# Second chunk's y read with its tokens regrouped, turned into a whole tile, and fetched back in four loads

## The chip, the cores and the metric

One core of a Trainium2 chip runs the kernel. The metric is device time in microseconds for one execution. The engines are TensorE (PE in the profile, its weight loads PEld), VectorE (DVE), ScalarE (ACT), GpSimd (POOL) and SyncE (SP, which in this kernel issues all DMA transfers). They run side by side, each in its own program order, and wait for one another through semaphores.

## The reference

A token mixer (sliding-window attention) times a gate from an MLP, over 2048 tokens of 512 features, all in float32:

```python
x = A_x                                   # 1 x 2048 x 512
xn = _layernorm(x, axis=-1)
s = _A_ref(xn, A_wqkv, A_wo)              # 32 heads of 16, window of 256 tokens, softmax, @ wo
g = _silu(_B_ref(xn, B_w1, B_b1, B_w2, B_b2))
return x + s * g

def _B_ref(x, w1, b1, w2, b2):
    y = _layernorm(x, axis=-1)
    h = _gelu(jnp.einsum("bsd,df->bsf", y, w1) + b1)      # 512 -> 1792
    return jnp.einsum("bsf,fd->bsd", h, w2) + b2          # 1792 -> 512
```

## The kernel before

**Stages.** The first 432 us or so are attention: 128 steps over 8 groups of heads and 16 blocks of keys, with the projections and the first chunk's hidden layer filled in between. Attention's unnormalised result goes to DRAM as `oT_d` (with the row of sums that the softmax divides by). Then the MLP and the output run over four chunks of 512 tokens. Chunks 0 and 1 are the loop `for c in range(2)`; chunks 2 and 3 are worked out together behind it, by another scheme.

**float32 products.** A product of two float32 matrices is made of three passes on TensorE: each operand is split into a high part and the rest (`gh` and `gl`, `yh` and the part in `xnT`, and so on). `split` makes them: a cast on ScalarE (or VectorE), then a subtraction on VectorE that needs the cast.

**The loop of a chunk.** Its 14 steps go over the 14 tiles f of 128 hidden units (in chunk 0 in the order 2, 3, 0, 1, 4, 5, 6 ... 13). In step i, ScalarE applies the gelu to tile `order[i]` and casts it to `gh`, VectorE subtracts for `gl` (`activate`, `split_g`), and PE projects the tile of the step before: four groups of `gh` x high, `gh` x low, `gl` x high (`project`, 12 matmuls into `acc`). `gh` and `gl` have two buffers each. In chunk 0 most hidden tiles exist already: 2, 3, 0 and 1 on the chip, 6 to 13 in DRAM (`h_d`, fetched as `hr`); 4 and 5 are made in the loop (`hidden`). The loop also settles late weights (`late_w`: casts and subtractions of `w` and `wos`, by the table `LATE`). After step 14 `end_chunk` adds the bias, applies the SiLU to `gated`, multiplies attention's four tiles `ohl` with `wos` on PE (48 matmuls `s`), and writes x + s * g out.

**y for the second chunk.** The MLP's input must stand with features in partitions and tokens along the row. Normalised x is in DRAM as `xn_d` (8 blocks of 128 tokens). Ahead of the loop, four loads bring chunk 1's blocks 4 to 7 into `y_1_0` ... `y_1_3` (pool `yp`, four buffers). In step 3 VectorE takes their statistics and POOL the power -1/2; in step 4 ScalarE normalises them in place, then `turn_y` transposes each tile on VectorE in place, in squares of 32 x 32, and sends it to DRAM (`z_d`). In step 5 `fetch_y` gathers for each quarter kt of the features four bands of 32 partitions: in each row, 16 pieces of 32 tokens, 128 bytes each. These 16 transfers land in `mlp["yy"][1][kt]` (part of `xnT`). Step 12 splits kt = 0 (its high part goes to `yh`), step 13 kt = 1, step 14 the other two. Chunk 1's hidden layer starts right behind `end_chunk`.

**Attention's tiles.** `fetch_sums` loads the softmax sums (`den`), steps 4 and 5 take reciprocals of them in four parts, step 5 writes them to DRAM (`rden_d`) and then calls `load_o` four times: a raw tile `or` of 8 heads (from `oT_d`, 8 slabs of 16 rows of 2 KB, into the buffers of pool `yp`) and its reciprocals, the `rec` (from `rden_d`, 8 rows, each repeated for 16 partitions; into a spare part of the `w2` area, in the profile `w`). Steps 9 to 12 multiply the two, steps 10 to 13 split the product into `ohl`.

**Order.** All engines but SP keep the order in which the program issues (`Ordered`), so every instruction carries line 43 in the profile, and tiles are told apart by their names. Inside the loop SP keeps that order too (`nc.sync.on = True`); elsewhere a scheduler may reorder SP. Eight semaphores serve SP's transfers in turn, so that one is issued only when the eighth before it has landed. DRAM areas are `dram.tile`s; a transfer that reads one waits for the ones that wrote it.

**Where in the code.** The loads of `y_1` are in line 872, `turn_y` in line 887, `fetch_y` in 894, `load_o` in 901, the loop from line 1081, step 4's transposes, step 5's transfers and the table of the splits from line 1124. Buffer `wa` of pool `bigp` holds `g_first` (the first two gelu tiles) until step 2 and `gated` from the end of chunk 0.

Of the kernel before, what the change touches and what calls it, by code (L numbers as in the profile page):

```python
# [9 lines left out]
F32 = mybir.dt.float32  # L10
# [7 lines left out]
S, D, H, DH, WIN, F = 2048, 512, 32, 16, 256, 1792  # L18
P = 128
NCH = S // 512  # L20
# [30 lines left out]
def mixer_kernel(ctx, tc, x, wqk, wv, wo, w1, b1, w2, b2, out):  # L51


    nc = SimpleNamespace(**{name: Ordered(tc, name) for name in ("tensor", "vector", "scalar", "gpsimd", "sync")})

    const = ctx.enter_context(tc.tile_pool(name="const", bufs=1))
    bigp = ctx.enter_context(tc.tile_pool(name="bigp", bufs=1))
    t2 = ctx.enter_context(tc.tile_pool(name="t2", bufs=5))
    small = ctx.enter_context(tc.tile_pool(name="small", bufs=3))
    dram = ctx.enter_context(tc.tile_pool(name="dram", bufs=1, space=bass.MemoryType.DRAM))  # L60
# [16 lines left out]
    def load(pool, tag, src, name, shape=(P, 512)):  # L77
        t = pool.tile(list(shape), F32, tag=tag, name=name)
        nc.sync.dma_start(t, src)
        return t  # L80
# [101 lines left out]
    xn_d = dram.tile([8, P, D], F32, name="xn_d")  # L182
    oT_d = dram.tile([4, 8, 32, S], F32, name="oT_d")
# [2 lines left out]
    w_d = {"w1": dram.tile([P, NF * 512], F32, name="w1_d"), "w2": dram.tile([P, NF * 512], F32, name="w2_d"),  # L186
           "wo": dram.tile([P, 4 * 512], F32, name="wo_d")}
    g_d = dram.tile([NF, P, 512], F32, name="g_d")
    z_d = dram.tile([NCH - 1, 4, P, 512], F32, name="z_d")
    mT_d = dram.tile([NQ, NCH, 32, P], F32, name="mT_d")  # L190


# [392 lines left out]
    mlp = {}  # L585
# [110 lines left out]
    n, raw = raws["qk"]  # L696
# [172 lines left out]
            nc.sync.dma_start(den[32 * g: 32 * g + 32], oT_d[g, :, DH].rearrange("a (c t) -> a c t", c=NCH))  # L869
        return den  # L870

    mlp["y"] = [load(mlp["yp"], "y", xn_d[4 + i], f"y_1_{i}") for i in range(4)]
    for f in range(6, NF, 2):
        t = gp.tile([P, 2, 512], F32, tag="ohl", name=f"hr_{f}", bufs=4)
        nc.sync.dma_start(t, h_d[f - 6: f - 4].rearrange("f p t -> p f t"))
# [11 lines left out]
    def turn_y(c, tiles):  # L887

        for i in tiles:
            y = mlp["y"][i]  # L890
            nc.vector.transpose(y, y)
            nc.sync.dma_start(z_d[c - 1, i], y)

    def fetch_y(c, kt, dst):

        for k in range(4):
            at = z_d[c - 1, 0, 0, 128 * kt + 32 * k: 128 * kt + 32 * k + 32]
            nc.sync.dma_start(dst[32 * k: 32 * k + 32].rearrange("p (t j) -> p t j", j=32),
                              bass.AP(tensor=at.tensor, offset=at.offset, ap=[[512, 32], [32 * 512, 16], [1, 32]]))

    def load_o(c, g):

        cols = slice(512 * c, 512 * (c + 1))
        pool, tag = (t2, "t2") if c else (mlp["yp"], "y")
        raw = load(pool, tag, oT_d[g, :, 0:DH, cols], f"or_{c}_{g}")
        rec = mlp["w2", g // 2][:, 512 * (14 + g % 2): 512 * (15 + g % 2)].bitcast(F32)
        nc.sync.dma_start(rec, bass.AP(tensor=rden_d.tensor, offset=rden_d.offset + 8 * g * S + 512 * c,
                                       ap=[[S, 8], [0, DH], [1, 512]]))
        return raw, rec

    def split_o(c, g, raw):
        ohl = gp.tile([P, 2, 512], F32R, tag="ohl", name=f"ohl_{c}_{g}", bufs=4)
# [168 lines left out]
    for c in range(2):  # L1081
        accs = open_accs(c)
        gs, os_, hs, wanted = {}, [], {}, []
# [22 lines left out]
        for i in range(NF + 1):  # L1106
            if i < NF:
                activate(order[i])
            if c and i in (1, 2, 6, 7):
                y_steps(6, 10)  # L1110
            if c and i >= 10 and i < 14:
                second_y(i - 10)
            if c and i == 14:
                kept["w"] = bigp.tile([P, 768], F32R, tag="wb1", name="wsh")
                combine_w(0)
            if c == 0:
                for kind, f in late_w[LATE[i]: LATE[i + 1]]:
                    settle(kind, f, nc.scalar.copy, nc.vector)
            if i >= 1:
                project(accs, [(order[i - 1], gs.pop(order[i - 1]))], order[0], order[-1])  # L1120
            if i + ahead < NF and order[i + ahead] not in made and order[i + ahead] > 1:
                hidden(order[i + ahead])
            if c == 0:
                if i == 3:
                    mlp["ln"] = layernorm(mlp["y"], "C1", True)
                    y_steps(0, 5)
                if i == 4:
                    y_steps(5, 10)
                    turn_y(1, range(4))
                if i in (4, 5):  # L1130
                    for j in (2 * i - 8, 2 * i - 7):
                        nc.vector.reciprocal(den[:, P * j: P * (j + 1)], den[:, P * j: P * (j + 1)])
                if i == 5:
                    nc.sync.dma_start(rden_d.rearrange("g a (c t) -> (g a c) t", c=NCH), den)
                    wanted += [load_o(0, g) for g in range(4)]
                    for kt in range(KT):
                        fetch_y(1, kt, mlp["yy"][1][kt].bitcast(F32))
                for kt in {12: (0,), 13: (1,), 14: (2, 3)}.get(i, ()):
                    split(mlp["yy"][0][kt], mlp["yy"][1][kt], mlp["yy"][1][kt].bitcast(F32))
            else:  # L1140
                steps2(i)
            k = i - o_from
            if 0 <= k - 2 - o_late < 4:
                os_.append(split_o(c, k - 2 - o_late, wanted[k - 2 - o_late][0]))
            if 0 <= k - 1 - o_late < 4:
                nc.vector.tensor_mul(wanted[k - 1 - o_late][0], *wanted[k - 1 - o_late])
            if c and 0 <= k < 4:
                wanted.append(load_o(c, k))
            if c == 0 and i == NF:
                mlp["y"] = load_y(2)  # L1150
            if c:
                if i in (2, 3, 7, 8):
                    turn_y(2 + i // 5, (0, 1) if i in (2, 7) else (2, 3))
                if i == 3:
                    mlp["y"] = load_y(3)
                    kept[0] = gated[:, 2:4]
                    kept[1] = bigp.tile([P, 2, 512], F32, tag="wb1", name="y2_21")
                    for kt in range(KT):
                        fetch_y(2, kt, kept[kt // 2][:, kt % 2])
                if i in (8, 9):  # L1160
                    for kt in (2 * i - 16, 2 * i - 15):
                        put("21" if kt > 1 else "11", kt % 2, kept[kt // 2][:, kt % 2])
                if i == 8:
                    fetch_second()
                if i == 12:
                    fetch_pair(0)
            if c and i in (0, 1, 5, 6):
                y_steps(5, 6)
# [110 lines left out]
    for i in range(NF):  # L1279
# [48 lines left out]
```

## Time and profile before

| | us |
|---|---|
| Time, median of 3 runs | 747.47 (745.95 to 747.61) |
| The profiled execution, its time | 746.98 |
| The profiled execution, span from first to last instruction | 745.2 |

| engine | busy, us | share of the span | instructions |
|---|---|---|---|
| PE | 728.8 | 98% | 7360 |
| PEld | 585.6 | 79% | 7360 |
| DVE | 516.5 | 69% | 790 |
| ACT | 440.1 | 59% | 744 |
| POOL | 297.5 | 40% | 644 |

TensorE's granted clock was 1.000 over the span, and 105.71 MB moved in 84,025 DMA packets.

How to read it: times count from the span's start. A row of a timeline has the start, the time from the first start to the last end of merged instructions, the engine, the operation, `out<-in` by the program's names, the number of instructions and, in brackets, the idle time before and who ended it. Rows with SPq are the issuing of transfers on SP, not the moving of data. A row of the windows has the length of the stretch, then for each engine busy time and instructions, then TensorE's clock, the share of the 16 DMA engines that were busy, and what they moved in GB/s. A row of the waits has who waited, for whom, the total, how often, and the longest.

### The profile page before, as it was taken

What the parts mean: (1) busy time and instruction counts of PE and PEld (TensorE: products, weight loads), DVE (VectorE), ACT (ScalarE), POOL (GpSimd) and SP (SyncE); (2) the same over time, 40 slices, a digit from 0 to 9 for tenths busy, and PEclk for the clock granted to TensorE, in tenths of its full rate; (3) what the DMA queues carried; (4) which work ended last, traced back from release to release, by engine and by line L of the source; (5) the groups of instructions that cost most, each with busy time, mean ns of one, the idle gap of its engine ahead of it and who ended that gap; (6) DMA issues with size and microseconds to landing.
All of it is one profiled execution on the core that took longest, in us unless ns stands there. A gap on an engine that the chain in (4) does not pass through costs nothing.

```text
span 745.2 us, 18812 instructions
## 1 busy us (share of the span) xinstructions
PE 728.8 (98%) x7360; PEld 585.6 (79%) x7360; DVE 516.5 (69%) x790; ACT 440.1 (59%) x744; POOL 297.5 (40%) x644
## 2 busy tenths in 40 slices
PE   8999999999999999999999999999999999999997
PEld 7886777777778887777776688788888888888886
DVE  6886777877766678887773567656658755676643
ACT  7757767867667676778877756443544734442001
POOL 7413757757666555767867700020102000001102
PEclk9999999999999999999999999999999999999999
DMA  8633355757555624646735385745453322253611
GB/s 289 192 71 77 86 137 149 210 151 194 142 133 153 154 71 149 163 129 165 201 103 161 92 286 201 198 143 194 110 108 113 96 88 74 69 181 117 214 55 56
DMA packets 84025, 105.71 MB, mean 142 GB/s; under 512 B 36640, under 2 KB 36896, under 8 KB 83936
## 3 DMA queue, kind: packets, MB, share of 16 engines
q1 hardware_dynamic: 83936, 104.50, 49.5%
q8 instruction: 58, 0.95, 0.5%
q14 instruction: 31, 0.25, 0.1%
HBM read 54.53 MB, written 32.77 MB: 117 GB/s over the span
## 4 chain that ended last, share of the span: by engine, by line
PE 86%; ACT 5%; DVE 3%; DMA 2%; issue 1%; POOL 1%; SPq 1%; DVEq 0%; ACTq 0%; POOLq 0%
PE fb L43 19%; PE acc L43 17%; PE zo L43 12%; PE stb L43 9%; PE p L43 9%; PE s L43 6%; PE h L43 6%; PE xy L43 5%; ACT pt L43 4%; PE pv L43 3%; POOL pt L43 1%; DVE xy L43 1%; SPq L43 1%; DMA w<-rden_d 1%; DMA xnT<-z_d 1%
## 5 line engine op out<-in xcount | busy, mean ns | idle before, releaser
L43 POOL TENSOR_SCALAR_AFFINE_SELECT pt<-pt 128x256 f32<-128x256 f32 x480 | 192.9, 425 | 133.7 <-ACT pt L43 131.7
L43 ACT ACTIVATE pt<-stb 128x768 f32<-128x768 f32 (+1 forms) x244 | 188.5, 773 | 62.4 <-PE stb L43 55.1
L43 DVE TENSOR_REDUCE mt<-xy 128x4 f32<-128x1024 f32 (+1 forms) x128 | 152.6, 1192 | 4.4
L43 DVE COPY_PREDICATED xy<-upper,zo 128x512 f32<-128x512 int32 x112 | 77.8, 695 | 70.6 <-PE xy L43 63.1
L43 POOL TENSOR_TENSOR xo<-xo,gated 128x512 f32<-128x512 f32 x15 | 19.9, 1330 | 236.9 <-DVE gated L43 195.5
L43 PE MATMUL fb<-xnT,wqb 64*128 64x512 f32 (+1 forms) x684 | 104.6, 397 | 0.2
L43 PE MATMUL zo<-pt,vt 128*17 128x128 f32 x2880 | 103.7, 275 | 0.3 <-POOL pt L43 0.3
L43 PE MATMUL stb<-qk 64*128 64x384 f32 (+1 forms) x488 | 97.1, 393 | 6.2 <-ACT pt L43 3.9
L43 PE MATMUL acc<-w,gh 128*128 128x512 f32 x320 | 98.6, 389 | 0.4 <-ACT gh L43 0.4
L43 PEld LDWEIGHTS stb<-qk 64*128 64x128 f32 x488 | 45.8, 183 | 51.5 <-ACT pt L43 46.3
L43 PEld LDWEIGHTS zo<-pt,vt 128*17 128x17 f32 x2880 | 67.5, 97 | 15.6 <-issue 6.3
L43 PEld LDWEIGHTS fb<-xnT,wqb 64*128 64x128 f32 (+1 forms) x684 | 64.7, 185 | 11.0 <-DVE pjr L43 1.4
L43 PEld LDWEIGHTS acc<-w,gh 128*128 128x128 f32 x320 | 60.0, 188 | 13.1 <-ACT gh L43 0.8
L43 PE MATMUL acc<-w,gl 128*128 128x512 f32 x160 | 62.3, 390 | 1.0 <-DVE gl L43 1.0
L43 PE MATMUL xy<-qk 64*128 64x256 f32 (+2 forms) x536 | 58.4, 291 | 0.2
L43 PEld LDWEIGHTS xy<-qk 64*128 64x128 f32 x536 | 46.6, 185 | 6.6 <-issue 3.1
L43 ACT COPY oraw<-zo 128x128 f32<-128x128 f32 x128 | 34.0, 266 | 29.4 <-PE zo L43 28.7
L43 PE MATMUL s<-wos,ohl 128*128 128x512 f32 (+1 forms) x204 | 44.3, 376 | 0.0
L43 ACT ACTIVATE gated<-acc 128x512 f32<-128x512 f32 x16 | 8.7, 596 | 59.3 <-DVE acc L43 59.3
L43 PEld LDWEIGHTS s<-wos,ohl 128*128 128x128 f32 x204 | 36.8, 188 | 7.1
L43 PEld LDWEIGHTS zo<-qk 64*128 64x128 f32 x448 | 38.5, 185 | 4.6 <-issue 1.4
L43 ACT COPY p<-p 128x512 f32<-128x512 f32 x21 | 12.3, 585 | 48.9 <-PE p L43 41.2
(191 smaller groups left out, 1233.8 us busy)
## 6 DMA issues: line engine op xcount, KB each, us to landing
qk<-sh SPq DMA_DIRECT2D x128, 128.0 KB
qk<-pjr SPq DMA_DIRECT2D x64, 128.0 KB
oT_d<-oraw SPq DMA_DIRECT2D x32, 256.0 KB
w_d<-in_w_dram SPq DMA_DIRECT2D x14, 512.0 KB
x<-in_x_dram SPq DMA_DIRECT2D x16, 256.0 KB
or<-oT_d SPq DMA_DIRECT2D x16, 256.0 KB
w<-rden_d SPq DMA_DIRECT2D x16, 256.0 KB
xo<-in_x_dram SPq DMA_DIRECT2D x16, 256.0 KB
```

Of the source, the lines that this page charges most:

```text
L43: r = issue(*args, **kwargs)
```

## The change

The four loads of `y_1` take other tokens together: tile i has rows 32 i to 32 i + 31 of each of the blocks 4 to 7, so that partition 32 a + t holds token 128 a + 32 i + t of the chunk. The four transposes write into one tile `whole`, in buffer `wa`, in which partition 32 a + p has, for each band b of 32 features, the 128 tokens of block a in a row. Four transfers, one for each a, write it to `zt_d`, whose rows are features and whose columns are tokens, in pieces of 128 tokens (512 bytes). Four whole loads of 128 rows of 2 KB bring `mlp["yy"][1]` back, in place of the 16 gathers.

SP's order in step 5 becomes: the four writes, the four raw tiles, `rden_d`, the four loads of y, the four `rec`. Before, it was the writes (in step 4), `rden_d`, raw and `rec` in turn four times, the 16 gathers. The split of kt = 0 moves from step 12 to step 9. Behind the loop, SP's built order mixes the next chunk's four `y` loads with the four `xo` loads (y, xo, y, xo, xo, y, xo, y; before, the four `y` came first). On ACT and DVE nothing else moves, and PE's and POOL's orders are as before. Chunks 2 and 3 use `turn_y` and `fetch_y` as before, with `z_d` now for two chunks.

```diff
-    z_d = dram.tile([NCH - 1, 4, P, 512], F32, name="z_d")
+    z_d = dram.tile([2, 4, P, 512], F32, name="z_d")
+    zt_d = dram.tile([S // 4, 512], F32, name="zt_d")
...
-    mlp["y"] = [load(mlp["yp"], "y", xn_d[4 + i], f"y_1_{i}") for i in range(4)]
+    mlp["y"] = [load(mlp["yp"], "y", xn_d[4: 8, 32 * i: 32 * i + 32], f"y_1_{i}") for i in range(4)]
...
-    def load_o(c, g):
-
-        cols = slice(512 * c, 512 * (c + 1))
+    def load_raw(c, g):
+
         pool, tag = (t2, "t2") if c else (mlp["yp"], "y")
-        raw = load(pool, tag, oT_d[g, :, 0:DH, cols], f"or_{c}_{g}")
+        return load(pool, tag, oT_d[g, :, 0:DH, 512 * c: 512 * (c + 1)], f"or_{c}_{g}")
+
+    def load_rec(c, g):
+
         rec = mlp["w2", g // 2][:, 512 * (14 + g % 2): 512 * (15 + g % 2)].bitcast(F32)
         nc.sync.dma_start(rec, bass.AP(tensor=rden_d.tensor, offset=rden_d.offset + 8 * g * S + 512 * c,
                                        ap=[[S, 8], [0, DH], [1, 512]]))
-        return raw, rec
+        return rec
+
+    def load_o(c, g):
+        return load_raw(c, g), load_rec(c, g)
...
                 if i == 4:
                     y_steps(5, 10)
-                    turn_y(1, range(4))
+                    whole = bigp.tile([P, 16, 4, 32], F32, tag="wa", name="y_1")
+                    for j, y in enumerate(mlp["y"]):
+                        nc.vector.transpose(whole[:, :, j], y.rearrange("p (b t) -> p b t", t=32))
...
                 if i == 5:
+                    for a in range(4):
+                        nc.sync.dma_start(zt_d[:, P * a: P * (a + 1)].rearrange("(b p) t -> p b t", p=32),
+                                          whole[32 * a: 32 * a + 32].rearrange("p b i t -> p b (i t)"))
+                    first_o = [load_raw(0, g) for g in range(4)]
                     nc.sync.dma_start(rden_d.rearrange("g a (c t) -> (g a c) t", c=NCH), den)
-                    wanted += [load_o(0, g) for g in range(4)]
                     for kt in range(KT):
-                        fetch_y(1, kt, mlp["yy"][1][kt].bitcast(F32))
-                for kt in {12: (0,), 13: (1,), 14: (2, 3)}.get(i, ()):
+                        nc.sync.dma_start(mlp["yy"][1][kt].bitcast(F32), zt_d[P * kt: P * (kt + 1)])
+                    wanted += [(first_o[g], load_rec(0, g)) for g in range(4)]
+                for kt in {9: (0,), 13: (1,), 14: (2, 3)}.get(i, ()):
                     split(mlp["yy"][0][kt], mlp["yy"][1][kt], mlp["yy"][1][kt].bitcast(F32))
```

More of the change, by code (lines that the diff above doesn't have):

```diff
@@ L891, in turn_y @@
             nc.vector.transpose(y, y)
-            nc.sync.dma_start(z_d[c - 1, i], y)
+            nc.sync.dma_start(z_d[c - 2, i], y)
     def fetch_y(c, kt, dst):
         for k in range(4):
-            at = z_d[c - 1, 0, 0, 128 * kt + 32 * k: 128 * kt + 32 * k + 32]
+            at = z_d[c - 2, 0, 0, 128 * kt + 32 * k: 128 * kt + 32 * k + 32]
             nc.sync.dma_start(dst[32 * k: 32 * k + 32].rearrange("p (t j) -> p t j", j=32),
                               bass.AP(tensor=at.tensor, offset=at.offset, ap=[[512, 32], [32 * 512, 16], [1, 32]]))
-    def load_o(c, g):
-        cols = slice(512 * c, 512 * (c + 1))
+    def load_raw(c, g):
         pool, tag = (t2, "t2") if c else (mlp["yp"], "y")
-        raw = load(pool, tag, oT_d[g, :, 0:DH, cols], f"or_{c}_{g}")
+        return load(pool, tag, oT_d[g, :, 0:DH, 512 * c: 512 * (c + 1)], f"or_{c}_{g}")
+    def load_rec(c, g):
         rec = mlp["w2", g // 2][:, 512 * (14 + g % 2): 512 * (15 + g % 2)].bitcast(F32)
```

## The prediction, made before the changed kernel ran

> **What bounds the kernel now.** I read the page first (busy time, chain of waits), then the timeline of PE around the change.
>
> ```profile
> span 745.2 us, 18812 instructions
> PE 728.8 (98%) x7360; PEld 585.6 (79%) x7360; DVE 516.5 (69%) x790; ACT 440.1 (59%) x744; POOL 297.5 (40%) x644
> ...
> PE 86%; ACT 5%; DVE 3%; DMA 2%; issue 1%; POOL 1%; SPq 1%; DVEq 0%; ACTq 0%; POOLq 0%
> ```
>
> PE is busy for 98% of the span, so the change can win only where PE waits, and lose wherever it makes PE wait. The timeline of PE in the loop of the first chunk (c = 0):
>
> ```profile
> 446.16 0.61 PE L43 MATMUL acc<-w,gh 128*128 128x512 f32 x2
> ...
> 452.05 0.39 PE L43 MATMUL acc<-w,gl 128*128 128x512 f32 x1
> ...
> 465.65 0.39 PE L43 MATMUL acc<-w,gl 128*128 128x512 f32 x1
> ...
> 473.88 0.73 PE L43 MATMUL acc<-w,gh 128*128 128x512 f32 x2 [0.36 <-ACT gh L43]
> 475.60 0.50 PE L43 MATMUL acc<-w,gl 128*128 128x512 f32 x1 [0.98 <-DVE gl L43]
> ...
> 478.00 11.04 PE L43 MATMUL s<-wos,ohl 128*128 128x512 f32 x48
> ```
>
> Each f takes twelve matmuls, one every 0.227 us (the 48 of 11.04 us), so 2.72 us; the third one needs gl. From 446.16 eleven such groups follow (f = 1, 4, 5, ... 13). Without waits the last would end at 446.16 + 11 x 2.72 = 476.1; the `s` matmuls start at 478.0. PE loses 1.9 us, all at f = 13. The timeline of ACT names the cause, the arrival of the second chunk's turned y (lines of 128 bytes from z_d):
>
> ```profile
> 471.93 0.62 ACT L43 CAST yh<-xnT 128x512 fp32r<-128x512 f32 x1 [3.37 <-DMA xnT<-z_d]
> ```
>
> ACT and DVE run in order, so gh and gl of f = 13 stand behind this cast and its subtraction. **The most that the change can win is therefore these 1.9 us.**
>
> **What is removed.** SP's timeline shows what was queued, in order:
>
> ```profile
> 430.11 0.52 SPq L43 DMA_DIRECT2D oT_d<-oraw  x1
> ...
> 431.42 2.61 SPq L43 DMA_DIRECT2D y<-xn_d  x4
> ...
> 437.42 2.84 SPq L43 DMA_DIRECT2D den<-oT_d  x4
> 440.32 1.04 SPq L43 DMA_DIRECT2D hr<-h_d  x2
> ...
> 443.88 1.76 SPq L43 DMA_DIRECT2D wos<-wo_d  x4
> 447.10 2.44 SPq L43 DMA_DIRECT2D z_d<-y  x4
> 453.69 0.32 SPq L43 DMA_DIRECT2D rden_d<-den  x1
> ...
> 461.19 15.22 SPq L43 DMA_DIRECT2D xnT<-z_d  x16
> ```
>
> Sixteen reads, 15.2 us of SP, become four, at the 0.44 us of one wos load some 1.8 us. If the four land before the casts at i = 13 and 14, the wait at f = 13 goes: minus 1.9.
>
> **What is moved at the front: the y loads.** Same four transfers of 256 KB, but each now gathers 32 rows from each of four slabs (4 x 32 x 512) instead of 128 rows in a line. The trace before has reads of such a shape: or<-oT_d and w<-rden_d gather 16 rows from each of eight slabs. Busy time by windows (the last two columns are the share of the 16 DMA engines, and GB/s):
>
> ```profile
> 447.50:451.50 4.00, 4.00 (x19) 3.31 (x18) 4.00 (x7) 3.29 (x6) 0.00 (x0) 1.00 1.05 400
> 461.25:462.25 1.00, 1.00 (x6) 0.81 (x5) 0.82 (x2) 0.29 (x1) 0.00 (x0) 1.00 0.47 180
> 497.00:498.00 1.00, 1.00 (x6) 0.80 (x6) 0.02 (x1) 0.00 (x0) 0.90 (x1) 1.00 0.50 190
> 474.00:477.00 3.00, 2.02 (x8) 1.36 (x9) 2.96 (x6) 1.19 (x2) 0.00 (x0) 1.00 0.80 125
> ```
>
> With whole 128-row transfers queued (447.5) all engines work, at 400 GB/s. With only eight-slab reads queued, several at once, half of them work, at 180 to 190. So eight slabs go to eight engines, the same eight for each transfer. I take it that four slabs go to four engines, a quarter of the rate: 262 KB at 100 GB/s is 2.62 us a load instead of 0.66. The only four-slab transfer in the rows, oT_d<-oraw, speaks for it: SP waits for it before den, so 256 KB took from 430.11 to 437.4. The bounds for the four loads are 2.6 us (all engines) and 10.5 us; I take 10.5, **7.9 us later** for the last.
>
> The row shows eight slabs only; from it alone the four loads might run on four different quarters, side by side, and cost nothing (first rival, 745.6). [...]
>
> Who waits: DVE's statistics of y at i = 3, with gl of f = 4 and all else queued behind them. SP's waits between 430 and 450, then DVE, then POOL:
>
> ```profile
> SPq L43 <- DMA y<-xn_d: 0.2, 1, 0.2
> ```
>
> ```profile
> 441.77 0.66 DVE L43 BATCH_NORM_STATS2 bnC<-y 128x6 f32<-128x512 f32 x1
> ...
> 442.68 0.17 DVE L43 TENSOR_SCALAR veC<-mvC 128x4 f32<-128x4 f32 x1
> 444.11 0.69 DVE L43 TENSOR_TENSOR gl<-g,gh 128x512 fp32r<-128x512 f32 x1 [1.26 <-ACT gh L43]
> ...
> 445.32 0.15 DVE L43 SCALAR_TENSOR_TENSOR shiftC<-mvC,rsC 128x4 f32<-128x4 f32 x1
> 446.36 2.83 DVE L43 STREAM_TRANSPOSE y<-y 128x512 f32<-128x512 f32 x4 [0.89 <-ACT y L43]
> ...
> 450.76 0.63 DVE L43 TENSOR_TENSOR gl<-g,gh 128x512 fp32r<-128x512 f32 x1
> ...
> 461.91 0.69 DVE L43 TENSOR_TENSOR or<-or,w 128x512 f32<-128x512 f32 x1 [0.18 <-issue]
> 463.15 0.69 DVE L43 TENSOR_TENSOR gl<-g,gh 128x512 fp32r<-128x512 f32 x1 [0.55 <-ACT gh L43]
> ```
>
> ```profile
> 442.94 1.02 POOL L43 TENSOR_TENSOR rsC<-veC,mhalf 128x4 f32<-128x4 f32 x1 [16.33 <-DVE veC L43]
> ```
>
> SP's short wait on a y load ended just before it issued hr at 440.32; one load further (0.66) the last y was in, about 441.0, at the latest 441.77. With 7.9 more: T = 448.9. The chain from there, by these rows' distances: veC at T + 0.9, the power on POOL done at T + 2.2, gl of f = 4 and the subtraction of w (444.11 to 445.32, 1.2 us) meanwhile, the shift at T + 2.3 = 451.2 instead of 445.32, 5.9 late. The normalisation on ACT, the four transposes, the reciprocals and gl of f = 5 follow without a gap to give way: gl starts at 456.7, is done at 457.3, and PE wanted it at 452.05. **First stall: 5.2 us** (4.4 to 6.0 with the landing between 0.8 earlier and later).
>
> **The transposes** (0.71 us each) now write sixteen blocks of 128 bytes at a stride instead of in place. No row shows that; from no difference up to twice the time (2.8 us, all on the chain above). I take none: element count and engine are the same. The buffer of `whole` held g_first, last read by PE long before; the next owner, gated, is written after 478. Both free.
>
> **The writes.** Pieces of 512 bytes, 1 MB in all. 128-byte pieces run at 125 GB/s with the engines 0.80 busy, 2 KB pieces at 400: 1 MB is 8.4 us by the one and 2.6 by the other. In time of one engine a piece costs 0.80 x 16 x 128 B / 125 GB/s = 13 ns and 1.05 x 16 x 2048 B / 400 GB/s = 86 ns; a straight line between gives 28 ns for 512 bytes, 2048 pieces on 16 engines **3.5 us**. [...]
>
> **SP's new order.** The raws pass rden_d, but the reciprocals' loads (rec, w<-rden_d) now stand behind the four y reads, which stand behind the landing of the writes. The first rec releases or_0's product, at i = 9, and gl of f = 10 is queued behind it. On the four slow engines, after T = 448.9: hr 2.1 MB, den 0.26, b2s 0.26, wos 1.05, 3.7 MB at 400 GB/s 9.2 us; the writes 3.5; four raws at 185 GB/s (eight slabs) 5.7; rden_d 0.7; y reads 2.6; the first rec 1.4. That ends at 472.0. The chain of waits has what a landing takes beyond its data:
>
> ```profile
> 453.69 1.98 DMA rden_d<-den
> ...
> 455.68 6.14 DMA w<-rden_d
> ```
>
> rden_d, 0.66 of data, took 1.98; half of the 1.3 beyond comes after the data: rec lands at 472.6 instead of about 461.8. Product (0.6) and gl (0.7) end at 473.9. PE wants gl of f = 10 at 465.65 + 5.2 = 470.9. **Second stall: 3.0 us**; from 0 (a queue 3 us shorter) to 7.9 (writes at the 128-byte price, 4.9 more).
>
> **The split moved from i = 12 to i = 9** (one ACT cast, one DVE subtraction): its y is in at about 469.5, three us after ACT wants it, but gh of f = 10 is then done near 471.4, inside the second stall, so nothing on top. Were rec early, it would cost 0.6. At the loop's end the next chunk's x and xo loads go out in mixed order; the 11 us of `s` matmuls hide them, without that cover 0.7 each.
>
> **Sum.** The profiled execution took 746.98 (span 745.2 and 1.8 around it), the median of the runs is 747.47, 0.5 above. 746.98 + 5.2 + 3.0 - 1.9 = 753.3; with the 0.5, **753.8**.
>
> **Rivals.**
> 1. The four loads spread over all engines, or over different quarters: place, the statistics of y at i = 3; price, nothing in place of 8.2. It decides if the last y lands by 443.7 (a shift up to 0.66 late is free, since gl of f = 5 was done at 451.4 and wanted at 452.05). Only the gain stays: 747.47 - 1.9 = 745.6, not slower. For it: no row shows a four-slab read. Against it: 0.47 and 0.50.
> 2. Only the first stall: the queue is 3 us shorter and rec arrives in time. 747.47 + 5.2 - 1.9 = 750.8. For it: engines other than the four slow ones have room. Against: a transfer lands when its slowest engine is done.
> 3. The 512-byte writes cost as much per byte as 128-byte pieces: second stall 7.9, 758.7. For it: 125 GB/s is the only row with small pieces. Against: those are reads, 16 engines only 0.80 busy.
>
> **How the numbers follow.** Forecast 0.53, rival 1 0.12, rival 2 0.18, rival 3 0.17. A change under 0.3% (2.2 us) can't be told from none here. Rival 1's 1.9 lies just within that: 0.07 same, 0.05 faster; the others, 0.88, are slower. The range runs from rival 2 with its early landing (750.8 - 0.8, rounded down) to rival 3: 749.8 to 758.7; it leaves out rival 1 and what goes past rival 3.
>
> **What would show it.** Right: during the y loads, the DMA share falls towards 0.25; the last statistics start near 449; PE waits for gl of f = 5 about 5 us; or_0's product waits for w<-rden_d; no wait is left at f = 13. Wrong: statistics near 442, or a first rec in before 465 with PE still late. The forecast fails altogether if four slabs do not mean four engines.

## The result, and the profile after

| | us |
|---|---|
| Before, median of 4 runs beside the changed kernel | 747.54 (745.95 to 748.28) |
| After, median of 4 runs | 757.30 (756.74 to 759.23) |
| Ratio, with its 95% interval | 1.0138 [1.0114, 1.0163] |
| The profiled execution after, its time | 756.74 |
| Its span | 755.0 |

The change makes the kernel slower by 9.8 us (1.4%). The prediction said 753.8 us. The page of the kernel after, the span, busy times and the chain of waits:

```profile
span 755.0 us, 18773 instructions
PE 733.9 (97%) x7360; PEld 588.5 (78%) x7360; DVE 517.4 (69%) x790; ACT 439.8 (58%) x744; POOL 297.9 (39%) x644
...
PE 82%; DMA 5%; ACT 4%; DVE 3%; issue 2%; POOL 2%; SPq 1%; DVEq 0%; ACTq 0%; POOLq 0%
...
PE fb L43 17%; PE acc L43 17%; PE zo L43 11%; PE p L43 9%; PE stb L43 9%; PE s L43 6%; PE h L43 5%; PE xy L43 5%; ACT pt L43 4%; PE pv L43 3%; DMA y<-xn_d 2%; SPq L43 1%; POOL pt L43 1%; DMA rden_d<-den 1%; DVE xy L43 1%
```

PE has the same 7360 matmuls, and its busy time grows by 5.1 us: some of them take longer. DMA's share of the chain went from 2% to 5%, with y<-xn_d and rden_d<-den now in it by name. The timeline of PE after, at the places where it waited in the loop of chunk 0:

```profile
451.00 0.50 PE L43 MATMUL acc<-w,gl 128*128 128x512 f32 x1 [2.02 <-DVE gl L43]
451.34 0.89 PE L43 MATMUL acc<-w,gh 128*128 128x512 f32 x2
...
456.26 0.73 PE L43 MATMUL acc<-w,gh 128*128 128x512 f32 x2 [1.11 <-ACT gh L43]
457.98 0.50 PE L43 MATMUL acc<-w,gl 128*128 128x512 f32 x1 [0.99 <-DVE gl L43]
...
475.50 0.79 PE L43 MATMUL acc<-w,gl 128*128 128x512 f32 x1 [2.03 <-DVE gl L43]
...
487.63 11.04 PE L43 MATMUL s<-wos,ohl 128*128 128x512 f32 x48
```

There are waits at f = 4 and 5 (451 to 458; I call them the first wait, after the first stall of the prediction), one at f = 10 (475.50, the second wait), and none at f = 13, where the kernel before lost 1.9 us. The `s` matmuls start at 487.63 instead of 478.00. What the waits end on, by the timelines of DVE and ACT after:

```profile
440.35 0.69 DVE L43 BATCH_NORM_STATS2 bnC<-y 128x6 f32<-128x512 f32 x1 [1.42 <-DMA y<-xn_d]
443.57 0.69 DVE L43 BATCH_NORM_STATS2 bnC<-y 128x6 f32<-128x512 f32 x1 [2.31 <-DMA y<-xn_d]
446.59 0.69 DVE L43 BATCH_NORM_STATS2 bnC<-y 128x6 f32<-128x512 f32 x1 [2.11 <-DMA y<-xn_d]
449.23 0.69 DVE L43 BATCH_NORM_STATS2 bnC<-y 128x6 f32<-128x512 f32 x1 [1.72 <-DMA y<-xn_d]
...
452.90 2.83 DVE L43 STREAM_TRANSPOSE y<-y 128x512 f32<-128x512 f32 x4 [0.88 <-ACT y L43]
...
457.29 0.63 DVE L43 TENSOR_TENSOR gl<-g,gh 128x512 fp32r<-128x512 f32 x1
...
474.15 0.69 DVE L43 TENSOR_TENSOR or<-or,w 128x512 f32<-128x512 f32 x1 [2.13 <-DMA w<-rden_d]
474.76 0.69 DVE L43 TENSOR_TENSOR gl<-g,gh 128x512 fp32r<-128x512 f32 x1
```

```profile
470.68 0.62 ACT L43 CAST yh<-xnT 128x512 fp32r<-128x512 f32 x1 [2.12 <-DMA xnT<-zt_d]
```

The four y tiles come in one after another, 2.6 to 3.2 us apart, the last at 449.23. The windows show what the DMA engines did meanwhile: three stretches after, in which SP had nothing issued behind the y loads (its next issue, hr, begins at 434.79 and is held until 439.8), then the stretch of the same loads before:

```profile
436.00:437.00 1.00, 1.00 (x6) 0.84 (x5) 0.61 (x2) 0.97 (x3) 0.00 (x0) 1.00 0.26 100
438.00:439.00 1.00, 1.00 (x6) 0.84 (x5) 0.93 (x2) 0.05 (x1) 0.00 (x0) 1.00 0.26 102
439.00:440.00 1.00, 1.00 (x7) 0.81 (x6) 0.00 (x0) 0.00 (x0) 0.00 (x0) 1.00 0.26 100
```

```profile
431.50:441.00 9.50, 9.50 (x44) 7.85 (x43) 6.30 (x13) 5.76 (x11) 0.00 (x0) 1.00 0.82 270
```

A share of 0.26 is the work of four of the 16 engines (0.26 x 16 = 4.2), at 100 GB/s together. Gl of f = 5 is queued behind their normalisation and starts at 457.29. At f = 10 gl is queued behind the first product of attention's tile, which waits for its `rec` until 474.15. The chain of waits names the transfers:

```profile
433.73 15.48 DMA y<-xn_d
...
462.39 7.66 DMA rden_d<-den
...
470.11 3.95 DMA w<-rden_d
```

The last y load took 15.48 us from issue to landing. `rden_d`, issued at 462.39 behind four raw tiles, landed 7.66 us later, and only then was the first `rec` issued. Besides the two waits there is a third cost, the clock. The windows after, behind the waits and between them (the column after POOL is TensorE's granted clock):

```profile
451.30:454.50 3.20, 3.20 (x9) 2.52 (x8) 2.01 (x5) 2.45 (x4) 0.52 (x1) 0.53 0.97 312
458.30:461.60 3.30, 3.30 (x9) 2.61 (x8) 3.03 (x5) 0.84 (x2) 0.00 (x0) 0.51 0.87 235
462.00:472.80 10.80, 10.80 (x49) 8.95 (x48) 4.57 (x7) 6.74 (x12) 0.00 (x0) 1.00 0.76 228
476.00:478.60 2.60, 2.60 (x7) 1.98 (x7) 2.56 (x5) 0.00 (x0) 0.00 (x0) 0.50 0.58 189
```

PE is busy all through 476.0 to 478.6 but does 7 matmuls, one in 0.43 us (476.10 to 476.95 is two), where 0.227 was the rule. The clock is halved three times for 3.4 us: behind the wait of 2.02 us, behind those of 1.11 and 0.99 us together, and behind that of 2.03 us. In the kernel before it stayed at 1.00 behind the wait of 0.98 us.

So the loss is made up like this. The first low product of f = 10 ran at 465.65 before and at 475.50 after, 9.85 us later. From there to `s` the kernel before took 12.35 us, of which 1.9 were waits at f = 13, so 10.45 without them. The kernel after has no wait there and takes 12.13 us: 1.9 less for the waits and 1.68 more. Nine matmuls behind the second wait, 475.50 to 479.20, account for the 1.68: they took 3.70 us, and at 0.227 each they would have taken 2.04. Together 9.85 - 1.9 + 1.68 = 9.63, the lateness of `s`.

### The profile page after: what moved, and what is told of

It reads as the page before. It is cut to its first block, busy times and chain, and to the rows that moved or that the text cites. A ratio compares the mean times of both kernels' runs of the same rounds, so it can differ in the third digit from the quotient of the medians.

```text
span 755.0 us, 18773 instructions
## 1 busy us (share of the span) xinstructions
PE 733.9 (97%) x7360; PEld 588.5 (78%) x7360; DVE 517.4 (69%) x790; ACT 439.8 (58%) x744; POOL 297.9 (39%) x644
## 4 chain that ended last, share of the span: by engine, by line
PE 82%; DMA 5%; ACT 4%; DVE 3%; issue 2%; POOL 2%; SPq 1%; DVEq 0%; ACTq 0%; POOLq 0%
PE fb L43 17%; PE acc L43 17%; PE zo L43 11%; PE p L43 9%; PE stb L43 9%; PE s L43 6%; PE h L43 5%; PE xy L43 5%; ACT pt L43 4%; PE pv L43 3%; DMA y<-xn_d 2%; SPq L43 1%; POOL pt L43 1%; DMA rden_d<-den 1%; DVE xy L43 1%
## 5 line engine op out<-in xcount | busy, mean ns | idle before, releaser
L43 PE MATMUL acc<-w,gh 128*128 128x512 f32 x320 | 102.1, 401 | 1.1 <-ACT gh L43 1.1
L43 PEld LDWEIGHTS acc<-w,gh 128*128 128x128 f32 x320 | 62.1, 194 | 14.9 <-ACT gh L43 1.8
L43 PE MATMUL acc<-w,gl 128*128 128x512 f32 x160 | 64.5, 403 | 5.0 <-DVE gl L43 5.0
L43 PEld LDWEIGHTS acc<-w,gl 128*128 128x128 f32 x160 | 31.3, 196 | 12.9 <-DVE gl L43 6.3
```

What stands on the lines that cost most here:

```text
L43: r = issue(*args, **kwargs)
```

## The experiments

Ratios are against the kernel before on the same chip, whose medians were 746.57 us for runs 1, 2, 4 and 5, 746.89 for 3, 6, 7 and 8, 746.85 for 9 to 11 and 746.70 for 12.

**1. Are the y loads slow because each uses four engines?** The loads in bands of 32 rows, 16 transfers in place of four.

```diff
-    mlp["y"] = [load(mlp["yp"], "y", xn_d[4: 8, 32 * i: 32 * i + 32], f"y_1_{i}") for i in range(4)]
+    mlp["y"] = [mlp["yp"].tile([P, 512], F32, tag="y", name=f"y_1_{i}") for i in range(4)]
+    for i in range(4):
+        for a in range(4):
+            nc.sync.dma_start(mlp["y"][i][32 * a: 32 * a + 32], xn_d[4 + a, 32 * i: 32 * i + 32])
```

> The changed kernel, but each regrouped load of y is cut into its four bands of 32 rows, sixteen transfers in place of four, none of which gathers from slabs. Theory (four slabs confine a load to four engines, which makes the last y late and all that is queued behind it): the last y is in near 441, the statistics start without waiting, both stalls go, and so does the halved clock behind them: 745.6 us (747.5 - 1.9), between 744.5 and 747.5. Rival A (the order of SP in step 5 makes the second stall by itself): the first stall goes, the second with its slow matmuls stays, 745.6 + 3.9 = 749.5. Rival B (the regrouped squares or the new transposes cost the time, however they are loaded): 757.

Measured 754.80 us, 1.0106 [1.0092, 1.0121]: a miss. The last y is in at 444.08 instead of 449.23 and the wait at f = 5 shrinks to 0.98 us, but the 16 transfers keep SP from 430.85 to 442.44 (before, the four took 2.61 us), and everything behind them is later. Now the split at step 9 waits 6.23 us for the turned y, and PE waits 3.73 and 2.32 us at f = 10, and the clock is at 0.50 in 473.4 to 477.4 (timelines of ACT and PE; the windows show the stretch behind the wait of 0.98 us at 452.83, in which the clock stays up, and the halved one):

```profile
468.15 0.62 ACT L43 CAST yh<-xnT 128x512 fp32r<-128x512 f32 x1 [6.23 <-DMA xnT<-zt_d]
```

```profile
470.09 0.73 PE L43 MATMUL acc<-w,gh 128*128 128x512 f32 x2 [3.73 <-ACT gh L43]
473.14 0.80 PE L43 MATMUL acc<-w,gl 128*128 128x512 f32 x1 [2.32 <-DVE gl L43]
```

```profile
452.90:456.00 3.10, 3.10 (x14) 2.42 (x15) 2.92 (x5) 0.89 (x2) 0.00 (x0) 1.00 0.98 305
473.40:477.40 4.00, 4.00 (x10) 3.13 (x11) 3.55 (x7) 0.00 (x0) 0.00 (x0) 0.50 0.65 210
```

It mixes the loads' shape with the cost of more transfers; the next runs part them.

**2. The four-slab loads alone**, everything else as before.

```diff
-    mlp["y"] = [load(mlp["yp"], "y", xn_d[4 + i], f"y_1_{i}") for i in range(4)]
+    mlp["y"] = [load(mlp["yp"], "y", xn_d[4: 8, 32 * i: 32 * i + 32], f"y_1_{i}") for i in range(4)]
```

> The kernel before with nothing changed but the four loads of y_1, which gather from four slabs (so the second chunk's MLP sees its tokens in another order, and that part of the output is not the reference's). Theory: the first stall comes whole, some 8.1 us with the slow matmuls behind it; the second not, since each rec follows its raw tile ahead of the reads of y; the wait at f = 13 stays or grows, as the reads queue later: 755.6 us, up to 758. Rival (the loads are harmless, the new writes, reads and order cost the time): 747.5.

This kernel leaves the rest of the change out, so the second chunk's MLP sees its tokens in another order; the amount of work is the same.

Measured 754.29 us, 1.0101 [1.0088, 1.0114]. One line of the diff, alone, costs 7.7 us; the whole change costs 9.8. (The parts don't add up: where the second wait follows, it takes up some of what the first one lost.) The loads come in slowly here too, their statistics starting at 441.00, 444.23, 447.16 and 449.66, and the DMA share in 436 to 448.8 is 0.53 (0.59 in the changed kernel). PE waits 2.01, 1.19 and 0.98 us at f = 4 and 5, as in the changed kernel.

**3. The same number of rows in sixteen slabs.** Each load gathers 8 rows from 16 places; here too the tokens stand in another order.

```diff
+    first = xn_d[4]
+    mlp["y"] = [load(mlp["yp"], "y", bass.AP(tensor=first.tensor, offset=first.offset + 8 * i * D,
+                                             ap=[[32 * D, 16], [D, 8], [1, D]]), f"y_1_{i}", (P, D))
+                for i in range(4)]
```

> The kernel before with only the four loads of y_1 changed, as in the run with the slab loads alone, but each gathers 8 rows from each of sixteen slabs in place of 32 from each of four (the second chunk's MLP sees its tokens in another order, and that part of the output is not the reference's). Theory (the number of slabs sets the number of engines): sixteen slabs use all engines, the last y is in near 441, no first stall: 746.6, the time of before on this chip, within 0.5. Rival (the gathering itself is slow, by shorter runs of rows in DRAM): 754 or more.

Measured 747.09 us, 1.0005 [0.9995, 1.0015]. Gathering costs nothing, the number of slabs does. The DMA engines work at 0.99 during the loads, where they had 0.26 to 0.33 in 436 to 440 with four slabs (the changed kernel), and the statistics in the timeline of DVE stand close together again:

```profile
436.00:441.00 5.00, 5.00 (x24) 4.14 (x23) 4.32 (x8) 2.61 (x6) 0.00 (x0) 1.00 0.99 295
```

```profile
439.53 0.69 DVE L43 BATCH_NORM_STATS2 bnC<-y 128x6 f32<-128x512 f32 x1 [0.18 <-DMA y<-xn_d]
...
442.35 0.68 DVE L43 BATCH_NORM_STATS2 bnC<-y 128x6 f32<-128x512 f32 x1
```

By the DMA share, and by 2.5 to 3.2 us from load to load in run 2 against 0.8 to 1.0 here, four slabs had the work of four engines and sixteen that of all 16; which four they are no run here shows.

**4. SP's old order in step 5, with the split back at step 12**, in the changed kernel.

```diff
-                    first_o = [load_raw(0, g) for g in range(4)]
                     nc.sync.dma_start(rden_d.rearrange("g a (c t) -> (g a c) t", c=NCH), den)
+                    wanted += [load_o(0, g) for g in range(4)]
...
-                    wanted += [(first_o[g], load_rec(0, g)) for g in range(4)]
-                for kt in {9: (0,), 13: (1,), 14: (2, 3)}.get(i, ()):
+                for kt in {12: (0,), 13: (1,), 14: (2, 3)}.get(i, ()):
```

> The changed kernel with the old order in step 5: after the writes, rden_d, then raw and rec in turn four times, then the four reads of y; the split of kt = 0 back in step 12. The four-slab loads stay. Theory (second stall = the first rec stands behind raws and reads on the four slow engines): the first rec lands near 466.5, the second stall and its slow matmuls (3.9 us) go, the reads land from 475 on, just in time for step 12: 757.3 - 3.9 = 753.4. Rival (the second stall comes from the backlog, whatever the order): 757.

Measured 755.03 us, 1.0115 [1.0098, 1.0133]. No wait at f = 10, but one of 0.88 us at f = 13, behind a cast that waits for the turned y until 479.22. The second wait and its half clock took 3.7 us (2.03 and 1.68), and `s` starts only 2.3 us sooner, at 485.33: some of the cost moves to the next wait.

**5. Whole loads with the change's other parts.** y in whole blocks, transposed to `whole[:, :, a]`; the columns of the second chunk are then regrouped, and the gelu of chunk 1 puts them back in order.

```diff
-    mlp["y"] = [load(mlp["yp"], "y", xn_d[4: 8, 32 * i: 32 * i + 32], f"y_1_{i}") for i in range(4)]
+    mlp["y"] = [load(mlp["yp"], "y", xn_d[4 + i], f"y_1_{i}") for i in range(4)]
...
+            if c:
+                nc.scalar.activation(g.rearrange("p (a j t) -> p j a t", a=4, j=4),
+                                     src.rearrange("p (j a t) -> p j a t", j=4, a=4),
+                                     AF.Gelu_apprx_tanh, bias=b1s[:, f: f + 1])
```

> A version meant to keep the gain without the slabs: y is loaded in whole rows as before the change, the transposes write whole[:, :, a] for block a, so that the same four transfers write pieces of 512 bytes in which the chunk's columns stand in another order; the second chunk's gelu reads its hidden tile in that order and writes it back in the tokens' own. Theory: no late y, no stall at the front; first rec near 462 to 464, at most 0.5 us late: 745.6 us, from 744.8 to 747. Rival A (second stall from the order): 749.5. Rival B (the gelu's reordered reading slows the second chunk): above 747.5 with no stall in the first chunk.

Measured 750.33 us, 1.0038 [1.0022, 1.0054]. The first wait is gone, and 6 us of the loss with it: 3.8 us above the kernel before instead of 9.8. But the `rec` is still late, with no backlog of y loads in front of it (timelines of DVE and PE):

```profile
467.97 0.69 DVE L43 TENSOR_TENSOR or<-or,w 128x512 f32<-128x512 f32 x1 [2.14 <-DMA w<-rden_d]
```

```profile
466.44 0.73 PE L43 MATMUL acc<-w,gh 128*128 128x512 f32 x2 [0.59 <-ACT gh L43]
469.32 0.50 PE L43 MATMUL acc<-w,gl 128*128 128x512 f32 x1 [2.15 <-DVE gl L43]
469.66 0.62 PE L43 MATMUL acc<-w,gh 128*128 128x512 f32 x2
470.12 0.40 PE L43 MATMUL acc<-w,gl 128*128 128x512 f32 x1
...
479.89 11.04 PE L43 MATMUL s<-wos,ohl 128*128 128x512 f32 x48
```

So SP's new order makes a second wait by itself, with whole loads in front of it. With the 0.59 us of the split at step 9 it is more than the 1.9 us that the change wins at f = 13: in the profiled execution `s` starts at 479.89, 1.9 us later than before. The span is 2.1 us longer than before, so the regrouped gelu of the second chunk costs at most the difference.

**6. The old order as well, and all splits at step 14.** Run 5 with the order of run 4 and this:

```diff
-                for kt in {12: (0,), 13: (1,), 14: (2, 3)}.get(i, ()):
+                for kt in {14: (0, 1, 2, 3)}.get(i, ()):
```

> The kernel of the run with regrouped columns (whole-row loads, writes in pieces of 512 bytes, four whole reads; 750.3), with the old order in step 5 (rden_d, then raw and rec in turn, then the four reads of y) and all four splits in step 14. Theory (what was left there, some 3 us and the clock behind it, came from the raw tiles and the reads standing ahead of the first rec): no stall at f = 10 and none at f = 13: 744.7. Rival A (the writes in pieces of 512 bytes hold the queue long enough to make the first rec late in any order): 748. Rival B (the gelu's reordered reading costs in the second chunk): 746 or above with no wait in the first.

Measured 746.89 us, 0.9999 [0.9990, 1.0007]. The wait at f = 13 is gone, yet the 1.9 us don't show: products of attention's tiles now wait for w<-rden_d, 1.89 us at 466.82 and 1.64 at 470.82, and PE 0.89 us behind the second of them, at f = 12. That the four whole reads of y take the room, since they are queued earlier than the 16 gathers were, is only read from the order; run 11 takes the next step.

**7. The splits at step 14 in the kernel before.** The same one-line edit there.

> The kernel before with one line changed: all four splits of the second chunk's y in step 14 (before: 12, 13, 14, 14). Theory (the wait at f = 13 is gh and gl queued behind a split whose y is late; nothing else needs that split before the next chunk): the 1.9 us at f = 13 go: 746.6 - 1.9 = 744.7. Rival (the wait moves to the bias addition and the end of the chunk, since ACT and DVE now have four splits in a row there): 746.6 or above.

Measured 748.46 us, 1.0013 [1.0002, 1.0025]. The wait moves on (timeline of PE): the `s` matmuls now wait in their middle for `gated`, whose bias stands behind the last splits on DVE.

```profile
475.95 5.60 PE L43 MATMUL s<-wos,ohl 128*128 128x512 f32 x24
483.91 7.36 PE L43 MATMUL s<-wos,ohl 128*128 128x512 f32 x24 [2.36 <-DVE gated L43]
```

**8. What is the half clock worth?** Run 4 with 28 spare products (matmuls into a bank that nothing reads) in PE's waits at f = 4 and 5, so that PE isn't idle.

```diff
+    WARM = {4: (0, 10), 5: (13, 5)}
+
+    def keep_busy(n):
+
+        if n:
+            spare = ps_yt.tile([P, 512], F32, tag="b", name="spare")
+        for _ in range(n):
+            nc.tensor.matmul(spare, w2_part(0, 2)[:, 0:P], w2_part(0, 2), start=True, stop=True)
...
+        keep_busy(warm[0])
...
+                    if k == 2 and i == 0:
+                        keep_busy(warm[1])
```

> The kernel of the run with the old order in step 5 (four-slab loads, first stall alone, 755.0), with matmuls into a spare bank that nobody reads, where PE waited: 10 ahead of the gl of f = 4, 13 ahead of f = 5, 5 ahead of its gl, 28 x 0.227 = 6.4 us, the length of the waits. Theory (a wait of about 2 us makes the granted clock fall to half for 3.4 us): the clock stays at 1.00 from 450 to 462, the nine matmuls behind the wait take 2.0 instead of 3.6 us: 755.0 - 1.6 = 753.4. Rival (the matmuls behind a wait are slow because data come late or memory is loaded, not by the clock): 755 or above.

Measured 756.25 us, 1.0127 [1.0106, 1.0148]: no gain. The matmuls did keep to one in 0.23 us up to 479.78, but PE then waited 1.77 and 0.99 us at f = 13 for the turned y, cast at 480.00 (479.22 in run 4), and took 0.43 us for each behind them (from 484.26 on), the pace of the half clock. What the full clock won ahead of it was waited away.

**9 and 10. The same in the changed kernel, once in the first waits, once in the second.** `WARM = {4: (0, 9), 5: (13, 5)}`, and `WARM = {10: (0, 9)}`.

> The changed kernel, whose TensorE is given spare products in its first waits: nine ahead of the low product of f=4, thirteen ahead of the products of f=5 and five ahead of its low product, all written to a bank of PSUM that nothing reads. In the changed kernel TensorE waited 2.02 us at 451.00, 1.11 us at 456.26 and 0.99 us at 457.98, and worked at half the clock in 451.3 to 454.5 and 458.3 to 461.6, which took some 1.7 us. Theory: the product of f=10 waits for w<-rden_d, which lands at 474.15 whatever TensorE does before, so that the time won by the full clock is waited away there: clock 1.00 up to 475, the wait before the low product of f=10 grows from 2.03 to about 3.7 us, and the time stays at 757.3 us. Rival: each half-clock stretch is time lost for good; then 757.3 less 1.7 = 755.6 us.

> The changed kernel with nine spare products ahead of the low product of f=10 alone, where TensorE waited 2.03 us at 475.50 and worked at half the clock for the 3.4 us behind it (0.50 in 476.0 to 478.6). Nine products of 0.227 us are 2.04 us, no more than the wait. Theory: behind this wait nothing holds TensorE up any more, so the full clock there is worth what the half clock took, 1.67 us: the products s begin at 486.0 instead of 487.63 and the time is 755.6 us. Rival: behind f=10 another wait sets the end (the low parts of f=11 to 13 or the split of the gathered squares), and the time stays at 757.3 us.

Measured 758.04 us, 1.0144 [1.0128, 1.0159], and 755.67 us, 1.0116 [1.0102, 1.0130]. With the first waits filled, PE waits 1.65 and 2.22 us at f = 10 instead of 2.03: the time won is waited away. (The profiled execution is the slowest of its four, 759.27 us, and there the first `rec` also lands 1.4 us later than in the changed kernel, so the two waits are not the gain alone.) With the second filled the clock is 1.00 in 476.0 to 478.6 (the timeline of PE, busy_second_wait; 0.50 in the same window of the changed kernel):

```profile
473.83 2.20 PE L43 MATMUL spare<-w 128*128 128x512 f32 x9
475.87 0.39 PE L43 MATMUL acc<-w,gl 128*128 128x512 f32 x1
...
486.30 1.98 PE L43 MATMUL s<-wos,ohl 128*128 128x512 f32 x8
```

475.87 + 10.45 = 486.32, so behind f = 10 nothing else holds PE up: from its first low product to `s` it takes 10.43 us instead of 12.13, which is the 1.7 us of the half clock. `s` itself comes 1.3 us sooner and the span is 1.3 us shorter, since that first product starts 0.37 us later. The medians differ by 1.6 us, but they are of two chips, and the intervals of the two ratios overlap; the trace carries the reading.

**11. Attention's tiles on sixteen engines.** Run 6 with the partitions of `or`, `rec` and the rows of `wo` in another order, so that the slowest dimension of each transfer has 16 parts and not 8.

```diff
-        return load(pool, tag, oT_d[g, :, 0:DH, 512 * c: 512 * (c + 1)], f"or_{c}_{g}")
+        return load(pool, tag, bass.AP(tensor=oT_d.tensor, offset=oT_d.offset + 256 * g * S + 512 * c,
+                                       ap=[[S, DH], [32 * S, 8], [1, 512]]), f"or_{c}_{g}")
...
-                                       ap=[[S, 8], [0, DH], [1, 512]]))
+                                       ap=[[0, DH], [S, 8], [1, 512]]))
...
-        fetch("wo", g)
+        nc.sync.dma_start(w_part("wo", 1, g).bitcast(F32),
+                          bass.AP(tensor=w_d["wo"].tensor, offset=w_d["wo"].offset + 512 * g,
+                                  ap=[[2048, DH], [2048 * DH, 8], [1, 512]]))
```

> columns_old_order with one thing more: the four loads or<-oT_d, the four loads w<-rden_d and the four of wo's rows run over the 16 dims of a head first and the 8 heads of a group behind them, instead of the 8 heads first (the same sums in another order of the partitions, in all four chunks). In columns_old_order the product or<-or,w waited 1.89 us for w<-rden_d at 466.82, 1.64 at 470.82 and 0.68 at 473.87, TensorE waited 0.89 us at 472.17, and the DMA share was 0.49 in 454 to 462, in which these loads ran: half of the 16 engines. Theory: a transfer whose slowest dimension has 8 parts runs on 8 engines, as the four-slab loads ran on 4; with 16 parts the waits for w<-rden_d go, TensorE's waits at f=10 and f=11 with them, some 1.3 us, and the time is 745.6 us. Rival: the transfers are held by what else is read in that stretch, or each row costs the same on whichever engine; then the time stays at 746.9 us.

Measured 745.25 us, 0.9975 [0.9965, 0.9985]. The windows of run 6, then of this run:

```profile
454.00:462.00 8.00, 8.00 (x37) 6.64 (x36) 4.95 (x9) 5.30 (x9) 0.00 (x0) 1.00 0.49 149
462.00:470.00 8.00, 8.00 (x37) 6.60 (x37) 4.47 (x8) 3.74 (x6) 0.00 (x0) 1.00 0.79 217
470.00:478.00 8.00, 7.08 (x30) 5.22 (x29) 6.42 (x12) 4.38 (x6) 0.00 (x0) 1.00 0.74 235
```

```profile
454.00:462.00 8.00, 8.00 (x37) 6.63 (x36) 4.97 (x9) 5.33 (x9) 0.00 (x0) 1.00 0.67 193
462.00:470.00 8.00, 8.00 (x37) 6.61 (x36) 6.35 (x12) 3.75 (x6) 0.00 (x0) 1.00 1.03 290
470.00:478.00 8.00, 8.00 (x37) 6.64 (x36) 7.54 (x13) 5.08 (x8) 0.00 (x0) 1.00 0.70 229
```

PE is busy all through 470 to 478, where it lacked 0.92 us, and the share of the DMA engines goes from 0.49 to 0.67 and from 0.79 to 1.03 while these loads run. No product waits for w<-rden_d any more, so these waits were engines left idle. (PE's wait of 0.89 us, which the expectation puts at f = 10 and 11, was at f = 12.)

**12. That alone, in the kernel before**, without the 512-byte pieces.

> The kernel before with the new order of the partitions alone: or<-oT_d, w<-rden_d and the rows of wo are loaded with the 16 dims of a head ahead of the 8 heads; y, its turned squares and the products of the second chunk are as before. It tells whether the time of heads_over_sixteen (745.25 us) needs the 512-byte pieces at all. Theory: the wait at f=13 in the kernel before came from the gathered squares landing at 472, behind the eight loads of or and w, the last of which landed near 471; on 16 engines these end near 468, the squares come in some 2 to 3 us earlier, and the wait at f=13, 1.67 us of time, goes: 745.2 us, so that the 512-byte pieces add nothing. Rival: the squares' sixteen loads of 128-byte pieces are issued one after another, some 0.5 us apart, and the last still land near 476; then the wait stays and the time is 746.9 us.

Measured 745.00 us, 0.9971 [0.9961, 0.9981]. It beats both kernels with y loaded, turned and gathered as before. The split of step 12 now has its data in time (its cast starts at 468.35 and waits for nothing, where the kernel before waited until 471.93), and `s` starts at 475.96, 2.0 us sooner. The 512-byte pieces add nothing to it.

## Why the prediction was right, and where it was short

The direction and the two waits came as forecast; the sum was 3.4 us short (753.3 for the profiled execution, measured 756.74).

- **Gain at f = 13**: no wait is left there in the changed kernel. Right as a row, and shown to be worth little by itself: run 6 has the gain without the two waits and is no faster than the kernel before.
- **Four slabs on four engines**: last y in at 449.23, forecast 448.9; the loads alone cost 7.7 us (run 2), and runs 2 and 3 show that the number of slabs is what costs. The sign that I had named, a DMA share towards 0.25, came while the y loads were alone: 0.24 to 0.33 in each us from 433 to 440, against 0.82 before. From 440 on it is 0.26 to 1.09, with hr and den beside them. That the landing came out to 0.3 us is partly luck: I counted 10.5 us of data for the four loads, and from the first issue (430.91) to the last landing they took 18.3.
- **First wait**: gl of f = 5 was to be done at 457.3; PE resumed at 457.98. Right in its cause; 0.3 of the lateness is the landing, 0.4 the power on POOL, 1.39 us for 1.02. What the forecast left out is the half clock behind it: PE came to the first low product of f = 10 at 473.47, 7.8 us later than before, where 5.2 were forecast.
- **Transposes**: 2.83 us for four, as before. Right.
- **Writes of 512 bytes**: a little dearer than forecast. The kernel after has a stretch with hardly anything but these writes under way, 458.00 to 459.00 (381 of its 389 packets are under 2 KB): 208 GB/s at a DMA share of 0.83. At that rate 1 MB takes 5.0 us; forecast were 3.5, by rival 3's price 8.4, by the rate of 2 KB pieces 2.6. In time of one engine a piece costs 0.83 x 16 x 512 B / 208 GB/s = 33 ns, where the straight line gave 28.
- **Second wait**: mis-sized. The product of the first `rec` was to start at 472.6 and started at 474.15; PE resumed at 475.50 instead of 473.9, 1.6 us later. In the trace `rec` isn't issued until `rden_d` has landed, at 470.05 (forecast 468.0), and takes 3.95 us from there. The term that was too short is the queue from the first write of y to the landing of the first `rec`: forecast 14.5 us (458.1 to 472.6), measured 18.3 (455.75 to 474.06). That the writes went out 2.3 us sooner than forecast hid most of it, by luck. Of the 3.8 us the writes can account for 1.5. I also laid the wait to the backlog of the four engines. Run 5 shows that it is there without the backlog: the same stretch takes 18.2 us (449.70 to 467.88, `rden_d` 7.67 of them), and PE resumes at 469.32, where the kernel before ran its gl of f = 10 at 465.65. The first rival's price, 745.6, was therefore wrong: with loads spread over all engines the other parts of the change cost 750.33.
- **Split at step 9**: cast at 470.68, inside the second wait, nothing on top. Right.
- **The missing term**: the sum had matmuls at 0.227 us throughout. Behind the wait at f = 10 the half clock took 1.68 us, and run 10 shows that this is lost for good. The same behind the first wait is not lost on top of it, as f = 10 resumes when `rec` lands (run 9). 1.6 + 1.68 = 3.28 of the 3.4 us.

Rival 3's 758.7 us is nearer to the result than the forecast, but the writes of 512 bytes were 1.5 us dearer than forecast and not 4.9, and most of the lateness has other causes. Rival 2, only the first wait, is closest to run 4 in its form, but its price was too low, again by the half clock: in run 4 PE resumes f = 5 at 458.39, 6.3 us late, works at the pace of the half clock for 3.4 us behind it (0.43 us a matmul), and still waits 0.88 us at f = 13: 755.03, not 750.8. What is shown for the second wait is SP's order: `rden_d` is 7.7 us on its way behind the four raw tiles (kernel after and run 5), while in run 6, with the same writes and the old order, the first `rec` is issued 2.5 us after `rden_d` and its product starts 12.5 us after the first write, without waiting. How the 18.2 us of the new order divide among the raw tiles, `rden_d`, the reads of y and `rec` was not parted further.

## What to carry to other kernels

Count the parts of a transfer's slowest dimension before regrouping what it loads: four parts cost 7.7 us here where sixteen cost nothing, and giving sixteen parts to loads that had eight won 1.6 and 1.7 us (runs 11 and 12), nearly the 1.9 that the change could have won. A wait that falls away is worth only the distance to the next one (f = 13 gave 1.9 us to the row and nothing to the time in runs 6 and 7), so look at what is due just behind it first. And price a wait of 2 us on TensorE with the half clock that may follow it, 1.7 us here, where nothing later will absorb it.

## What the hardware showed that was not expected

- **The clock after a short wait.** Waits of 0.98 us left the clock at 1.00 (kernel before, and run 1 at 452.83). Behind 2.02 us, behind 1.11 and 0.99 us together, and behind 2.03 us it was 0.50 to 0.53 for 3.4 us each (kernel after), 1.7 us lost each time.
- **In the kernel after, idle time seems to count by fixed stretches of 3.41 us, not by waits.** It is shown in windows of 3.41 us (the second number of a row is the time that PE was busy):

```profile
448.11:451.52 3.41, 1.39 (x6) 0.85 (x5) 2.22 (x5) 0.00 (x0) 1.09 (x1) 1.00 0.79 271
451.52:454.94 3.42, 3.42 (x9) 2.35 (x8) 2.23 (x5) 2.89 (x5) 0.30 (x1) 0.50 0.95 302
454.94:458.35 3.41, 1.31 (x5) 0.63 (x5) 3.41 (x6) 3.35 (x7) 0.00 (x0) 1.00 0.96 304
458.35:461.76 3.41, 3.41 (x10) 2.65 (x9) 2.98 (x5) 0.79 (x2) 0.00 (x0) 0.50 0.87 230
```

The half clock begins at 451.52, 458.35 and 475.41, 6.83 and 17.06 us apart, twice and five times 3.41, and in the 3.41 us ahead of each PE was idle for 2.02, 2.10 and 1.94 us (472.00 to 475.41 has 1.47 us busy, and the clock is 0.50 in 475.41 to 478.82). The half clock can last longer: in run 9 it was 0.50 in 476.0 to 478.6 and 0.73 in 478.6 to 486.0, 6.6 us at half in all. In the kernel before, 1.35 us of idle time in 472.69 to 476.10 (in it the waits of 0.36 and 0.98 us) left the clock at 1.00. So two short waits counted as one here, 1.11 and 0.99 us. In run 5 the rows go on at 0.23 us behind 0.59 and 2.15 us. That a wait counts for less where a boundary falls into it would fit, but it is a guess that no trace here shows: run 5's record of the clock stands at 0.95 throughout. The other executions of run 5 part in two: 747.35 to 748.03 us at a mean clock of 0.998 to 1.000, and 750.33 to 752.03 at 0.994 to 0.997.
- **Busy work paid only at the last wait here.** 28 and 27 spare products kept the matmuls at 0.23 us (run 8) and the clock at 1.00 (run 9, 452 to 463) behind the first waits and won nothing (1.0127 against 1.0115 in run 4, 1.0144 against 1.0138), as a later wait took it up; nine in run 10 won 1.3 us of the profiled span.
